# Weight words two pieces at a time, and eight of block 1's first products inside block 0's stage

## The chip, the cores and the metric

The kernel runs on one core of one Trainium2 chip. The metric is device microseconds for one execution, on that core. The core has a matrix engine (TensorE, in the trace PE, with its weight loads as PEld), a vector engine (VectorE, DVE), a scalar engine (ScalarE, ACT), GpSimd (POOL) and an engine that issues the data transfers (SyncE, SP). Each works through its own instructions in order, and semaphores tie them together.

## The reference

The input `x` is 2 sequences of 4096 tokens with 192 features. Three steps follow one another:

```
out = einsum('hk,bskhg->bshg', softmax(weight), windows of 7 tokens of x)   # causal convolution, 8 heads of 24
g, val = x @ w_gate, x @ w_val                                              # 192 -> 1536
x = (g * sigmoid(g) * val) @ w_out                                          # 1536 -> 192
h = x @ w_in                                                                # 192 -> 2048
g = where(h > 0, h, exp(min(h, 0)) - 1)
out = g @ w_out2                                                            # 2048 -> 192
```

The activations are float32; the five weight matrices of the two layers come as float64, that is as 64-bit words.

## The kernel before, in words

**Tiling.** The 8192 tokens are 16 blocks of 512. A block goes through layer 1 (gate, value, out) as one stage and through layer 2 (in, out) as another. The stages run in the order (1,0), (1,1), (1,2), (2,0), (2,1), (1,3), (2,2), (1,4), (2,3) and so on, the first number being the layer, the second the block. There are 14 places where layer 1 hands over to layer 2.

**Products.** Every float32 operand is split into a high and a low part of the type fp32r, and a product is the sum of three partial ones. The 192 rows of the contraction are handled as three slots of 64, and the matmuls go out in couples, one on the lower and one on the upper 64 rows. A unit of layer 1 (12 to a block) is `nine`: 18 matmuls of line 362 into the PSUM banks pg and pv. Then come silu of pg (ACT, line 672), the gate product with pv (DVE, line 676), the high part of the result (ACT, line 646) and its low part (DVE, line 650), which are called h. Then `ten`, 10 matmuls of line 405, adds h times the out weights into four banks c. In layer 2 a pair of units is one `nine` into two banks ph, with tanh and exp (ACT, lines 706 and 710), `less` and `bound` (DVE, lines 714 and 718), and the two parts of h for each of the two. pg, pv and ph share four PSUM banks (the ring "a"), so the `nine` after next writes the banks that silu and the gate product, or `bound`, must have read. The h parts have five buffers each.

Below, "OUT 3" is `ten` of unit 3 of a block, and a "first product" is a `nine`.

**Weights.** There are 34 pieces of 128 x 384 words. Pieces 0, 1, 3, 4, 6, 7, ... (12 of them) hold the gate and value columns of one unit of layer 1 (in1), pieces 2, 5, 8, ... the out rows of two units, and those from 18 on belong to layer 2. An in1 piece comes by four DMAs (line 262), as its upper and lower 64 rows have to change places; an out piece by one. Then ACT scales the high words (line 266) and takes the top bits of the low ones (line 289), DVE joins them and adds the sign (lines 293 and 274), ACT casts the high part (line 298) and DVE subtracts it for the low part (line 301). The words land in a ring `ws` of 4 buffers. A first product waits for both parts of its piece.

**Convolution.** For 128 of the 192 features a block's convolution is one multiply on ACT and six taps of 128x512 on DVE (line 576), then the split (lines 449 and 453). The last 64 features of blocks 0 and 1 go over PE (`pc`, line 552); from block 2 on, they are six more DVE taps of 128x256. The second copy of x with its halves turned around is made by DMAs (lines 490 and 496, issued on SP). Operands x and y live in three homes, each a pair of tiles for the high and the low part.

**Order.** The program lists every instruction as a task with a cost and what it needs. PE's tasks keep the order in which they were listed; on the other engines a planner picks, among the tasks that could start within 0.05 us of the first, the one with the longest work behind it. In the main loop a list `due` holds the units whose `ten` hasn't been listed: after each `nine`, all but the last entry of the list are worked off, so that OUT runs two units (or, in layer 2, two pairs) behind. At the end of a layer 1 stage the list is held for one step, and two OUTs follow after the first `nine` of layer 2.

Of the kernel before, what the change touches and what calls it, by code (L numbers as in the profile page):

```python
# [8 lines left out]
I32 = mybir.dt.int32  # L9
F32R = mybir.dt.float32r  # L10
# [6 lines left out]
P = 128  # L17
HALF = 64
TB = 512
SLOTS = (0, 2, 1)  # L20
LEAD = 3
AIDED = 1
PATIENCE = 0.05
EPS = 2.0**-16
SPARED = range(0, 34)

# [106 lines left out]
def tile_conv_swiglu_elu(ctx: ExitStack, tc: tile.TileContext, x, weight, words, out, FF1, FF2):  # L133
# [5 lines left out]
    nc = tc.nc  # L139
# [4 lines left out]
    NU = {1: FF1 // P, 2: FF2 // P}  # L144
    assert D == P + HALF and TB % 2 == 0
    C = 2 * D
# [5 lines left out]
    x_p = ctx.enter_context(tc.tile_pool(name="xp", bufs=1))  # L152
# [15 lines left out]
    plan = Plan()  # L168
# [10 lines left out]
    def move(emit, needs=(), new=(), uses=(), pitch=0.62, ready=2.9):  # L179
        return plan.add("sp", pitch, ready, emit, needs, new, uses)  # L180
# [65 lines left out]

    ready = {}

    def piece(k, moves, halves, serves):

        st_b, f_b = plan.buffer("ws", 4), plan.buffer("wf", 4)
# [10 lines left out]
        def scale():  # L264
            box["f"] = f = wf_p.tile([P, C], F32, tag="wf", name=f"w{k}")
            nc.scalar.activation(out=f, in_=box["st"][:, :, 1].bitcast(F32), func=AF.Abs, scale=2.0**-112)  # L266

# [16 lines left out]
        def three():  # L284

            w = box["st"].bitcast(U32)[:, :, 0]
            nc.scalar.activation(out=w, in_=w, func=AF.Copy, scale=2.0**-29 * (1 - EPS), bias=7.5 * EPS - 0.5)  # L289

# [12 lines left out]
        came = [  # L303
            move(lambda i=i: bring(i), new=[st_b] if i == 0 else (), uses=[] if i == 0 else [st_b], ready=3.3)
            for i in range(len(moves))
        ]
        for i in came[1:]:
            i.behind.append(came[0])
        t = act(scale, came, new=[f_b], uses=[st_b], pitch=0.45, ready=0.6)
        if k in SPARED:  # L310
            low_t = act(three, came, uses=[st_b], pitch=0.45, ready=0.6)
# [15 lines left out]
            ready[u] = his, los  # L327
        return came

    every, lower, upper = slice(0, P), slice(0, HALF), slice(HALF, P)  # L330

    class Into:


# [7 lines left out]
        def load(self, k, i):  # L342
            moves = (
                ((lower, slice(0, 3, 2)), (lower, slice(0, 3, 2))),
                ((lower, slice(1, 2)), (upper, slice(0, 1))),
                ((upper, slice(0, 3, 2)), (upper, slice(1, 3))),
                ((upper, slice(1, 2)), (lower, slice(1, 2))),
            )
            flat = lambda w: w[:, k].rearrange("p s c -> p (s c)")
            return piece(i, moves, [(lambda f: f, flat(self.hi), flat(self.lo))], [(self.name, k)])  # L350

        def nine(self, bufs, ps, k, x, n):

# [263 lines left out]
    live = {}  # L617
    parts = {}
    split_of = {}
    sums = {}  # L620
    turns = {"last": None}

# [10 lines left out]
    def split(u):  # L633

        layer, b, j = u
        n = blocks[b][2]
        t_b, done = live[u][1:]
        bufs = [plan.buffer(f"h{q}", 5) for q in ("hi", "lo")]
        parts[u] = [None, None]

        def make(q):
            parts[u][q] = h_p.tile([P, TB], F32R, tag=f"h{'hi lo'.split()[q]}", name=f"h{q}_{layer}_{b}_{j}")
# [12 lines left out]
        l = dve(lo, [done, h], new=[bufs[1]], uses=[bufs[0], t_b])  # L655
        split_of[u] = bufs, (h, l)
# [169 lines left out]
    products(1)  # L826
    load_table(AF.Silu)

    due = []
    for i, (layer, b) in enumerate(stages):  # L830
        if i + 1 < len(stages) and stages[i + 1][0] == 1:
            if i:
                load_x(stages[i + 1][1])
            conv(stages[i + 1][1], 0)
            if i >= AIDED:
                conv(stages[i + 1][1], 1)
        if i and stages[i - 1][0] != layer:
            load_table(AF.Silu if layer == 1 else AF.Exp)
        for j in range(0, NU[layer], layer):
            swiglu(b, j) if layer == 1 else elus(b, j // 2)  # L840

            hold = layer == 1 and j == NU[1] - 1 and i + 1 < len(stages) and stages[i + 1][0] == 2
            while len(due) > 1 and not hold:
                for u in due.pop(0):
                    products_out(u)
            due.append([(layer, b, j + a) for a in range(layer)])
    for us in due:
        for u in us:
            products_out(u)

    plan.run({"pe": 1.0, "act": 0.8, "dve": 1.0, "pool": 2.3, "sp": 0.8}, PATIENCE)


# [43 lines left out]
```

## Time and profile before

| | us |
|---|---|
| three runs of the kernel before | 1224.43 to 1225.32, median 1224.89 |
| the execution that was profiled | 1225.62 |
| its span, first to last instruction | 1223.9 |
| PE busy in the span | 1207.8 (99%) |
| DVE busy | 981.4 (80%) |
| ACT busy | 833.7 (68%) |

The profile comes from a single execution, with a span 1.72 us shorter than its device time. Times in the trace count from the first instruction of the span. The granted TensorE clock over the whole span was 0.997 of full speed. A matmul's row gives the time from its start to its modelled end; matmuls are pipelined, so that what counts is the distance between starts.

### The profile page before, as it was taken

What the parts mean: (1) busy time and instruction counts of PE and PEld (TensorE: products, weight loads), DVE (VectorE), ACT (ScalarE), POOL (GpSimd) and SP (SyncE); (2) the same over time, 40 slices, a digit from 0 to 9 for tenths busy, and PEclk for the clock granted to TensorE, in tenths of its full rate; (3) what the DMA queues carried; (4) which work ended last, traced back from release to release, by engine and by line L of the source; (5) the groups of instructions that cost most, each with busy time, mean ns of one, the idle gap of its engine ahead of it and who ended that gap; (6) DMA issues with size and microseconds to landing.
All of it is one profiled execution on the core that took longest, in us unless ns stands there. A gap on an engine that the chain in (4) does not pass through costs nothing.

```text
span 1223.9 us, 25338 instructions
## 1 busy us (share of the span) xinstructions
PE 1207.8 (99%) x10272; PEld 968.8 (79%) x10272; DVE 981.4 (80%) x1631; ACT 833.7 (68%) x1556; POOL 2.1 (0%) x15
## 2 busy tenths in 40 slices
PE   7999999999999999999999999999999999999998
PEld 5778888888888888788887888878878788888876
DVE  7999899788595986959779596895968869495697
ACT  6979687486583856748576484765848667485676
POOL 0000000000000000000000000000000000000000
PEclk9999999999999999999999999999999999999999
DMA  6644020202020020201102011020200102000000
GB/s 174 192 128 125 15 44 14 66 18 53 1 44 27 18 53 8 49 15 25 47 10 48 14 36 36 18 53 1 44 14 18 40 1 47 12 18 14 18 11 18
DMA packets 34917, 48.65 MB, mean 40 GB/s; under 512 B 5872, under 2 KB 19696, under 8 KB 34800
## 3 DMA queue, kind: packets, MB, share of 16 engines
q1 hardware_dynamic: 34784, 47.04, 15.1%
q8 instruction: 80, 1.31, 0.5%
q14 instruction: 37, 0.30, 0.1%
q10 hardware_dynamic: 16, 0.00, 0.0%
HBM read 19.75 MB, written 6.29 MB: 21 GB/s over the span
## 4 chain that ended last, share of the span: by engine, by line
PE 92%; DVE 3%; ACT 2%; SPq 1%; DMA 1%; issue 1%; ACTq 0%; DVEq 0%
PE c L405 40%; PE pv L362 30%; PE ph L362 21%; DMA words<-in_words_dram 1%; SPq L262 1%; DVE t L714 1%; DVE t L718 1%; PE pg L362 0%; DVE w L293 0%; DVE h L650 0%; ACT w L266 0%; DVE t L676 0%; ACT words L289 0%; SPq L518 0%; DVE in1lo L301 0%
## 5 line engine op out<-in xcount | busy, mean ns | idle before, releaser
L405 PE MATMUL c<-h,out 64*128 64x512 f32 x4480 | 639.4, 392 | 0.5 <-DVE o L755 0.4
L405 PEld LDWEIGHTS c<-h,out 64*128 64x128 f32 x4480 | 472.9, 185 | 104.6 <-DVE o L755 4.1
L646 ACT CAST h<-t 128x512 fp32r<-128x512 f32 x448 | 278.7, 623 | 175.3 <-DVE t L676 126.8
L362 PE MATMUL pg<-x,in1hi 64*128 64x512 f32 x1152 | 391.0, 393 | 2.9 <-ACT in1hi L298 2.3
L362 PE MATMUL pv<-x,in1hi 64*128 64x512 f32 x1152 | 391.1, 393 | 0.8 <-DVE t L676 0.8
L650 DVE TENSOR_TENSOR h<-t,h 128x512 fp32r<-128x512 f32 x448 | 307.6, 687 | 93.9 <-ACT h L646 91.2
L362 PE MATMUL ph<-y,in2hi 64*128 64x512 f32 x1536 | 317.6, 391 | 0.0
L362 PEld LDWEIGHTS ph<-y,in2hi 64*128 64x128 f32 x1536 | 236.7, 185 | 35.5 <-DVE t L718 0.6
L362 PEld LDWEIGHTS pv<-x,in1hi 64*128 64x128 f32 x1152 | 213.2, 185 | 49.3 <-DVE t L676 1.2
L362 PE MATMUL ph<-y,in2lo 64*128 64x512 f32 x768 | 238.3, 391 | 0.0
L362 PE MATMUL pg<-x,in1lo 64*128 64x512 f32 x576 | 226.7, 394 | 2.0 <-DVE in1lo L301 2.0
L676 DVE TENSOR_TENSOR t<-t,pv 128x512 f32<-128x512 f32 x192 | 131.3, 684 | 119.2 <-ACT t L672 119.0
L362 PE MATMUL pv<-x,in1lo 64*128 64x512 f32 x576 | 226.7, 394 | 0.0
L362 PEld LDWEIGHTS pg<-x,in1hi 64*128 64x128 f32 x1152 | 213.3, 185 | 7.5 <-ACT in1hi L298 4.1
L672 ACT ACTIVATE t<-pg 128x512 f32<-128x512 f32 x192 | 114.4, 596 | 148.1 <-PE pg L362 145.9
L714 DVE SCALAR_TENSOR_TENSOR t<-t,th 128x512 f32<-128x512 f32 x256 | 175.2, 685 | 9.8 <-ACT t L710 9.1
L718 DVE SCALAR_TENSOR_TENSOR t<-ph,t 128x512 f32<-128x512 f32 x256 | 171.8, 686 | 3.0
L706 ACT ACTIVATE th<-ph 128x512 f32<-128x512 f32 x256 | 153.7, 600 | 24.1 <-PE ph L362 23.1
L362 PEld LDWEIGHTS ph<-y,in2lo 64*128 64x128 f32 x768 | 141.2, 185 | 16.5
L710 ACT ACTIVATE t<-ph 128x512 f32<-128x512 f32 x256 | 154.0, 601 | 0.0
L362 PEld LDWEIGHTS pv<-x,in1lo 64*128 64x128 f32 x576 | 106.7, 185 | 24.4
L362 PEld LDWEIGHTS pg<-x,in1lo 64*128 64x128 f32 x576 | 106.7, 185 | 5.4 <-DVE in1lo L301 4.2
(56 smaller groups left out, 528.2 us busy)
## 6 DMA issues: line engine op xcount, KB each, us to landing
x<-x SPq DMA_DIRECT2D x64, 128.0 KB, 3.2
y<-y SPq DMA_DIRECT2D x64, 128.0 KB, 2.3
words<-in_words_dram SPq DMA_DIRECT2D x14, 384.0 KB, 3.4
words<-in_words_dram SPq DMA_DIRECT2D x40, 128.0 KB, 2.8
x<-x SPq DMA_DIRECT2D x64, 64.0 KB, 2.0
out_dram<-o SPq DMA_DIRECT2D x16, 256.0 KB, 2.0
xs<-in_x_dram SPq DMA_DIRECT2D x14, 259.0 KB, 3.1
words<-in_words_dram SPq DMA_DIRECT2D x40, 64.0 KB, 2.5
```

The source lines that it names most:

```text
L262: nc.sync.dma_start(out=to[r, g], in_=w[r_in, g_in])
L362: nc.tensor.matmul(p[:, :n], w[r, k, s], m[r, s, :n], start=i == 0, stop=i == len(seq) - 1)
L405: nc.tensor.matmul(p[:, :n], lhs[r], m[r, :n], start=start, stop=stop)
L646: nc.scalar.copy(parts[u][0][:, :n], live[u][0]["t"][:, :n])
L650: nc.vector.tensor_tensor(out=parts[u][1][:, :n], in0=live[u][0]["t"][:, :n], in1=raw(parts[u][0][:, :n]), op=ALU.subtract)
L672: nc.scalar.activation(out=box["t"][:, :n], in_=box["p"][0][:, :n], func=AF.Silu)
L676: nc.vector.tensor_tensor(out=t, in0=t, in1=box["p"][1][:, :n], op=ALU.mult)
L706: nc.scalar.activation(out=own["th"][:, :n], in_=box["p"][a][:, :n], func=AF.Tanh, scale=0.5)
L710: nc.scalar.activation(out=own["t"][:, :n], in_=box["p"][a][:, :n], func=AF.Exp)
L714: nc.vector.scalar_tensor_tensor(out=t, in0=t, scalar=1.0, in1=th, op0=ALU.add, op1=ALU.mult)
L718: nc.vector.scalar_tensor_tensor(out=t, in0=box["p"][a][:, :n], scalar=0.0, in1=t, op0=ALU.max, op1=ALU.min)
```

## The change

**Words by two.** The in1 pieces of the units 2 to 11 come in couples: a couple's words, 2 x 128 x 384, land by five DMAs in place of eight in one of the two tiles of the home that block 2's x will have, the couples taking turns between the two tiles. Both pieces of a couple wait for all five DMAs. Pieces 0 and 1 and the out pieces come as before.

**Block 1 in block 0's stage.** `both_first` lists the stages (1,0) and (1,1). Block 1's convolution is listed ahead of block 0's units. In block 0's stage OUT follows one `nine` behind. From unit 4 on (JOINED), each `nine` of block 0 is followed by one of block 1, so that units 0 to 7 of block 1 stand in block 0's stage. Their h parts don't go to the h ring but to the storage of in2's and out2's weights (`held`), and the pieces of layer 2 wait until those have been used (`give_back`). The transfer and convolution of block 2 are listed behind that. Then block 1's last four units follow, with two OUTs after each.

**Due.** `settle_due` works off at most two entries of the list after a `nine` of layer 1, and at most one after a `nine` of layer 2; an entry with a block's last unit ends the step.

```diff
+    def pair(k, which):
+        ring = ("xhi", "xlo")[which] + str(home["x", LEAD - 1])
+        st_b = plan.buffer(ring, 1)
...
+            at, r, g_in, row = (
+                (0, lower, 0, 0), (2, every, 2, 0), (0, upper, 1, HALF), (1, lower, 0, HALF), (1, upper, 1, 0)
+            )[i]
+            n = r.stop - r.start
+            source = words[k : k + 2, row : row + n, g_in * G2 : (g_in + 1) * G2].rearrange("e p c -> p e c")
+            nc.sync.dma_start(out=box["st"][r, :, at], in_=source)
...
+            if self.name == "in1" and k >= ALONE:
+                n, e = divmod(k - ALONE, 2)
+                if e == 0:
+                    self.pair = pair(i, n % 2)
+                shared = (*self.pair[:2], lambda view=self.pair[2]: view(e))
...
-        bufs = [plan.buffer(f"h{q}", 5) for q in ("hi", "lo")]
+        kept = u in held
+        bufs = [{"users": []} if kept else plan.buffer(f"h{q}", 5) for q in ("hi", "lo")]
...
+    for j in range(NU[1] - JOINED):
+        half = j // 2
+        held[1, 1, j] = (
+            ((spare[0][2], half), (spare[1][2], half)) if j % 2 == 0 else ((spare[2][2], j - 1), (spare[2][2], j))
+        )
...
+    def settle_due(most=2):
+
+        while len(due) > 1 and most:
+            us = due.pop(0)
+            for u in us:
+                products_out(u)
+            most = most - 1 if us[-1][2] < NU[us[-1][0]] - 1 else 0
+
+    def both_first():
+
+        conv(1, 0)
+        done = 0
+        waiting = []
+        for j in range(NU[1]):
+            swiglu(0, j)
+            if due:
+                for u in due.pop(0):
+                    products_out(u)
+            due.append([(1, 0, j)])
+            if j >= JOINED:
+                swiglu(1, done)
+                waiting.append([(1, 1, done)])
+                done += 1
+        load_x(2)
+        conv(2, 0)
+        conv(2, 1)
+        due.extend(waiting)
+        for j in range(done, NU[1]):
+            swiglu(1, j)
+            due.append([(1, 1, j)])
+            settle_due()
+
+    both_first()
     for i, (layer, b) in enumerate(stages):
+        if i < 2:
+            continue
...
-            while len(due) > 1 and not hold:
-                for u in due.pop(0):
-                    products_out(u)
+            if not hold:
+                settle_due(2 if layer == 1 else 1)
```

What moves on the engines is shown at three places. First DVE, from the low part of piece 0 (w0 is piece 0, w1 piece 1, w3 the piece of unit 2; cv1_0 is block 1's convolution, t1_0_0 unit 0 of block 0). Before:

```order
L301 TENSOR_TENSOR in1lo_115<-w0_189,in1hi_114 128x384
L576 SCALAR_TENSOR_TENSOR cv1_0_176<-xs1_143,taps_106,cv1_0_176 128x512
L477 TENSOR_TENSOR x11_243<-pc1_202,x10_235 64x256 x2
L301 TENSOR_TENSOR in1lo_115<-w1_216,in1hi_114 128x384
L293 SCALAR_TENSOR_TENSOR w3_250<-w3_250,words3_186 128x384
L274 SCALAR_TENSOR_TENSOR w3_250<-words3_186,w3_250 128x384
L576 SCALAR_TENSOR_TENSOR cv1_0_176<-xs1_143,taps_106,cv1_0_176 128x512
L301 TENSOR_TENSOR in1lo_115<-w3_250,in1hi_114 128x384
L576 SCALAR_TENSOR_TENSOR cv1_0_176<-xs1_143,taps_106,cv1_0_176 128x512 x2
L676 TENSOR_TENSOR t1_0_0_284<-t1_0_0_284,pv0_0_228 128x512
L576 SCALAR_TENSOR_TENSOR cv1_0_176<-xs1_143,taps_106,cv1_0_176 128x512
L650 TENSOR_TENSOR h1_1_0_0_317<-t1_0_0_284,h0_1_0_0_303 128x512
```

The same place now:

```order
L341 TENSOR_TENSOR in1lo_115<-w0_189,in1hi_114 128x384
L624 SCALAR_TENSOR_TENSOR cv1_0_176<-xs1_143,taps_106,cv1_0_176 128x512
L525 TENSOR_TENSOR x11_243<-pc1_202,x10_235 64x256 x2
L341 TENSOR_TENSOR in1lo_115<-w1_216,in1hi_114 128x384
L624 SCALAR_TENSOR_TENSOR cv1_0_176<-xs1_143,taps_106,cv1_0_176 128x512 x4
L730 TENSOR_TENSOR t1_0_0_277<-t1_0_0_277,pv0_0_228 128x512
L501 TENSOR_TENSOR x11_243<-cv1_0_176,x10_235 128x512
L704 TENSOR_TENSOR h1_1_0_0_304<-t1_0_0_277,h0_1_0_0_296 128x512
L333 SCALAR_TENSOR_TENSOR w3_301<-w3_301,words3_186 128x384
L312 SCALAR_TENSOR_TENSOR w3_301<-words3_186,w3_301 128x384
L730 TENSOR_TENSOR t1_0_1_314<-t1_0_1_314,pv0_1_271 128x512
```

All four remaining taps of block 1 (before: one, then two, then one, with piece 3 and the gate product between them) and the split of their sum now stand ahead of piece 3's join, and piece 3's low part has moved behind the second gate product.

Second, DVE in the middle of block 0's stage (t1_0_4 and t1_0_5 are units of block 0, w8 to w11 pieces). Before:

```order
L650 TENSOR_TENSOR h1_1_0_3_482<-t1_0_3_437,h0_1_0_3_469 128x512
L274 SCALAR_TENSOR_TENSOR w8_445<-words8_365,w8_445 128x384
L293 SCALAR_TENSOR_TENSOR w9_488<-w9_488,words9_390 128x384
L274 SCALAR_TENSOR_TENSOR w9_488<-words9_390,w9_488 128x384
L676 TENSOR_TENSOR t1_0_4_495<-t1_0_4_495,pv0_4_430 128x512
L301 TENSOR_TENSOR out1_118<-w8_445,out1_118 128x2x128
L301 TENSOR_TENSOR out1_118<-w8_445,out1_118 128x2x64
L301 TENSOR_TENSOR in1lo_115<-w9_488,in1hi_114 128x384
L293 SCALAR_TENSOR_TENSOR w10_530<-w10_530,words10_433 128x384
L274 SCALAR_TENSOR_TENSOR w10_530<-words10_433,w10_530 128x384
L650 TENSOR_TENSOR h1_1_0_4_560<-t1_0_4_495,h0_1_0_4_541 128x512
L676 TENSOR_TENSOR t1_0_5_546<-t1_0_5_546,pv0_5_485 128x512
```

Now, where t1_1_0 is unit 0 of block 1:

```order
L341 TENSOR_TENSOR out1_118<-w8_435,out1_118 128x2x64
L312 SCALAR_TENSOR_TENSOR w9_491<-words9_378,w9_491 128x384
L704 TENSOR_TENSOR h1_1_0_4_539<-t1_0_4_498,h0_1_0_4_524 128x512
L333 SCALAR_TENSOR_TENSOR w10_535<-w10_535,words9_378 128x384
L341 TENSOR_TENSOR in1lo_115<-w9_491,in1hi_114 128x384
L730 TENSOR_TENSOR t1_1_0_553<-t1_1_0_553,pv1_0_505 128x512
L312 SCALAR_TENSOR_TENSOR w10_535<-words9_378,w10_535 128x384
L333 SCALAR_TENSOR_TENSOR w11_567<-w11_567,words11_430 128x384
L312 SCALAR_TENSOR_TENSOR w11_567<-words11_430,w11_567 128x384
L730 TENSOR_TENSOR t1_0_5_589<-t1_0_5_589,pv0_5_542 128x512
L341 TENSOR_TENSOR in1lo_115<-w10_535,in1hi_114 128x384
L704 TENSOR_TENSOR in2lo_117<-t1_1_0_553,in2hi_116 128x512
```

A gate product and a low part of block 1 stand between those of block 0, and the low part's place is in2lo.

Third, PE where block 2 enters its layer 2, after the last couple of the first `nine` (ph2_0 and ph2_1; c1_3 are the banks of OUT for block 3's layer 1). Before, with two OUTs:

```order
L362 MATMUL ph2_1_3553<-y21_2305,in2hi_116 128x512
L405 MATMUL c1_3_2_3186<-h0_1_3_9_3499,out1_118 128x512
...
L405 MATMUL c1_3_3_3187<-h1_1_3_9_3507,out1_118 128x512
L405 MATMUL c1_3_2_3186<-h0_1_3_10_3536,out1_118 128x512
...
L405 MATMUL c1_3_3_3187<-h1_1_3_10_3544,out1_118 128x512
L362 MATMUL ph2_2_3609<-y20_2221,in2hi_116 128x512
```

Now:

```order
L410 MATMUL ph2_1_3517<-y21_2442,in2hi_116 128x512
L453 MATMUL c1_3_2_3153<-h0_1_3_9_3463,out1_118 128x512
...
L453 MATMUL c1_3_3_3154<-h1_1_3_9_3471,out1_118 128x512
L410 MATMUL ph2_2_3558<-y20_2225,in2hi_116 128x512
...
L410 MATMUL ph2_3_3559<-y21_2442,in2hi_116 128x512
L453 MATMUL c1_3_2_3153<-h0_1_3_10_3500,out1_118 128x512
```

One OUT stands between the first and the second `nine` of layer 2, where two stood; OUT 10 follows the second, and every later OUT of the stage stands one pair later than before. The last stage ends with eight OUTs behind its last `nine`, where six stood. At the step from layer 2 back to layer 1, four OUTs follow the first `nine` and two the second.

## Rows read from the trace of the kernel before

**Rows 1.** The page, part 1: busy us, share of the span, instructions per engine.
```profile
PE 1207.8 (99%) x10272; PEld 968.8 (79%) x10272; DVE 981.4 (80%) x1631; ACT 833.7 (68%) x1556; POOL 2.1 (0%) x15
```

**Rows 2.** Waits of PE: who waited for whom: us, times, longest us.
```profile
PE pg L362 <- ACT in1hi L298: 2.3, 3, 1.5
PE pg L362 <- DVE in1lo L301: 2.0, 5, 0.5
...
PE pv L362 <- DVE t L676: 0.8, 1, 0.8
PE pg L362 <- DMA x<-x: 0.5, 1, 0.5
```

**Rows 3.** Windows: length, busy us (instructions) by engine, PEclk, DMA share, GB/s.
```profile
core 0: us, PE busy (x) PEld busy (x) DVE busy (x) ACT busy (x) POOL busy (x), PEclk, DMA share, GB/s
15.40:31.20 15.80, 13.74 (x92) 10.19 (x92) 14.25 (x26) 10.07 (x23) 0.00 (x0) 0.89 0.66 179
16.30:19.60 3.30, 3.20 (x16) 2.63 (x17) 3.01 (x7) 1.85 (x5) 0.00 (x0) 0.50 0.75 167
31.20:74.70 43.50, 41.28 (x335) 31.45 (x337) 40.84 (x80) 37.39 (x79) 0.00 (x0) 1.00 0.54 153
50.00:60.00 10.00, 9.12 (x76) 6.72 (x74) 9.21 (x19) 9.24 (x21) 0.00 (x0) 1.00 0.75 218
74.70:152.00 77.30, 77.30 (x668) 62.54 (x666) 71.07 (x136) 58.38 (x120) 0.00 (x0) 1.00 0.34 94
152.00:231.00 79.00, 79.00 (x682) 63.72 (x680) 78.33 (x133) 59.87 (x114) 0.00 (x0) 1.00 0.18 43
74.70:1189.00 1114.30, 1114.30 (x9568) 896.93 (x9566) 887.13 (x1459) 752.72 (x1389) 0.13 (x2) 1.00 0.13 32
```

**Rows 4.** PE timeline of block 0: start us, us, line, [idle before <-releaser].
```profile
15.41 0.49 PE L362 MATMUL pg<-x,in1hi 64*128 64x512 f32 x1 [1.53 <-ACT in1hi L298]
...
23.10 0.49 PE L362 MATMUL pv<-x,in1hi 64*128 64x512 f32 x1 [0.77 <-DVE t L676]
...
25.06 1.56 PE L405 MATMUL c<-h,out 64*128 64x512 f32 x10
...
27.86 0.50 PE L362 MATMUL pg<-x,in1lo 64*128 64x512 f32 x1 [0.42 <-DVE in1lo L301]
```

**Rows 5.** DVE timeline from the first gate product on.
```profile
20.79 1.53 DVE L576 SCALAR_TENSOR_TENSOR cv<-xs,taps,cv 128x512 f32<-128x512 f32 x2
22.36 0.69 DVE L676 TENSOR_TENSOR t<-t,pv 128x512 f32<-128x512 f32 x1
22.96 0.75 DVE L576 SCALAR_TENSOR_TENSOR cv<-xs,taps,cv 128x512 f32<-128x512 f32 x1
23.73 0.69 DVE L650 TENSOR_TENSOR h<-t,h 128x512 fp32r<-128x512 f32 x1
...
25.11 0.56 DVE L293 SCALAR_TENSOR_TENSOR w<-w,words 128x384 int32<-128x384 int32 x1
25.70 0.56 DVE L274 SCALAR_TENSOR_TENSOR w<-words,w 128x384 int32<-128x384 int32 x1
```

**Rows 6.** SP timeline: DMA issues, start us, us, line, count.
```profile
15.78 1.87 SPq L496 DMA_DIRECT2D x<-x  x3
17.70 9.71 SPq L262 DMA_DIRECT2D words<-in_words_dram  x14
```

**Rows 7.** Timeline where block 2 enters its layer 2.
```profile
325.14 2.71 PE L405 MATMUL c<-h,out 64*128 64x512 f32 x20
...
327.46 0.61 PE L362 MATMUL ph<-y,in2hi 64*128 64x512 f32 x2
...
329.02 0.69 DVE L718 SCALAR_TENSOR_TENSOR t<-ph,t 128x512 f32<-128x512 f32 x1
```

**Rows 8.** Timeline after the last first product of layer 2.
```profile
1211.27 7.45 PE L405 MATMUL c<-h,out 64*128 64x512 f32 x60
...
1217.52 0.76 PEld L405 LDWEIGHTS c<-h,out 64*128 64x128 f32 x8 [0.26 <-DVE h L650]
```

More of the change, by code (lines that the diff above doesn't have):

```diff
@@ L23 @@
 PATIENCE = 0.05
+JOINED = 4
+ALONE = 2
 EPS = 2.0**-16
@@ L247, in tile_conv_swiglu_elu, with bring, piece @@
     ready = {}
-    def piece(k, moves, halves, serves):
-        st_b, f_b = plan.buffer("ws", 4), plan.buffer("wf", 4)
+    G2 = 2 * P
+    def pair(k, which):
+        ring = ("xhi", "xlo")[which] + str(home["x", LEAD - 1])
+        st_b = plan.buffer(ring, 1)
+        box = {}
+        def bring(i):
+            if i == 0:
+                full = x_p.tile([P, 3, TB], F32R, tag=f"x{which}{home['x', LEAD - 1]}", name=f"words{k}")
+                box["st"] = full.rearrange("p a b -> p (a b)").bitcast(I32).rearrange(
+                    "p (e g c) -> p e g c", e=2, g=3
+                )
[5 more added lines that the diff above has]
+            nc.sync.dma_start(out=box["st"][r, :, at], in_=source)
+        came = [
+            move(lambda i=i: bring(i), new=[st_b] if i == 0 else (), uses=[] if i == 0 else [st_b], ready=3.9)
+            for i in range(5)
+        ]
+        for i in came[1:]:
+            i.behind.append(came[0])
+        view = lambda e: box["st"][:, e].rearrange("p g (c w) -> p (g c) w", w=2)
+        return came, st_b, view
+    every, lower, upper = slice(0, P), slice(0, HALF), slice(HALF, P)
+    def piece(k, moves, halves, serves, shared=None):
+        st_b, f_b = shared[1] if shared else plan.buffer("ws", 4), plan.buffer("wf", 4)
         box = {}
@@ L264, in scale @@
         def scale():
+            if shared:
+                box["st"] = shared[2]()
             box["f"] = f = wf_p.tile([P, C], F32, tag="wf", name=f"w{k}")
@@ L284, in three @@
         def three():
+            if shared:
+                box["st"] = shared[2]()
             w = box["st"].bitcast(U32)[:, :, 0]
@@ L301, in lo_part @@
             nc.vector.tensor_tensor(out=lo, in0=pick(box["f"]), in1=raw(hi), op=ALU.subtract)
[L303 to L308, printed above, removed]
+        if shared:
+            came = shared[0]
+        else:
+            came = [
+                move(lambda i=i: bring(i), new=[st_b] if i == 0 else (), uses=[] if i == 0 else [st_b], ready=3.3)
+                for i in range(len(moves))
+            ]
+            for i in came[1:]:
+                i.behind.append(came[0])
         t = act(scale, came, new=[f_b], uses=[st_b], pitch=0.45, ready=0.6)
@@ L349, in load @@
             flat = lambda w: w[:, k].rearrange("p s c -> p (s c)")
-            return piece(i, moves, [(lambda f: f, flat(self.hi), flat(self.lo))], [(self.name, k)])
+            halves = [(lambda f: f, flat(self.hi), flat(self.lo))]
+            shared = None
+            if self.name == "in1" and k >= ALONE:
[3 more added lines that the diff above has]
+                shared = (*self.pair[:2], lambda view=self.pair[2]: view(e))
+            return piece(i, moves, halves, [(self.name, k)], shared)
         def nine(self, bufs, ps, k, x, n):
@@ L849, in tile_conv_swiglu_elu @@
             products_out(u)
+    give_back()
     plan.run({"pe": 1.0, "act": 0.8, "dve": 1.0, "pool": 2.3, "sp": 0.8}, PATIENCE)
```

23 lines of the change are left out of this document (22 added, 1 removed).

## The prediction

> **What bounds the kernel now.** I read the page first: PE is busy for 1207.8 of 1223.9 us [rows 1], so at most 16 us can be won without taking matmuls away, and the change takes none away. The windows say where these 16 us lie. From 74.70 to 1189.00 PE is busy without a break, 9568 matmuls at 0.1165 us each [rows 3]; there a change can only lose. Behind 1211.27 PE runs 60 matmuls, with 0.26 us of waiting [rows 8]. What is left is the start. From 15.40 to 31.20, 92 matmuls are worth 10.7 us and take 15.8, so 5.1 us are lost; from 31.20 to 74.70, 335 are worth 39.0 and take 43.5, so 4.5 are lost [rows 3]. These 9.6 us are what the change plays for.
>
> The table of PE's waits gives the causes by name: the high part of a weight piece 2.3 us, the low part 2.0, the gate product 0.8, the turned x 0.5 [rows 2]. They sum to 5.6, of which the 1.53 ahead of 15.41 lie outside the 9.6 [rows 4]; the remaining 5.5 are matmuls that start with a longer step though no wait is named. The largest such piece is the half clock: from 16.30 to 19.60 the granted clock is 0.50 (the 1.2 GHz level) and 3.3 us hold 16 matmuls [rows 3], where 0.1165 would allow 28; 12 x 0.1165 = 1.4 us. Behind the waits stands DVE: busy for 14.25 of the first 15.8 us and for 40.84 of the next 43.5 [rows 3]. Weight pieces, block 1's taps and the gate chain share it.
>
> **The start, to OUT 3.** Up to the low part of piece 1, the order of DVE and PE is as before, so PE's first two units and the half clock stay: from 15.41 on, part of their 36 matmuls run at half clock [rows 3], and they end at about 22, 6.5 us for 4.2, 2.3 lost. (In before unit 2 then waits for the gate product, to 23.10 [rows 4].)
>
> From there I chain by hand with the steps between starts on DVE: a tap behind its predecessor 0.78 (20.79 to 22.36 for two), a gate product 0.60 (22.36 to 22.96), a join with the sign behind it 0.59 (25.11 to 25.70) [rows 5]. Four taps, 3.1 us, now stand in one run ahead of the gate product of unit 0, where three taps and piece 3's join, sign and low part stood, 2.3 + 1.7. The gate product could come a little earlier for that; but its low part waits for ACT, which now casts x's split in front of it, and for DVE's own part of the split. I leave the gate product at 22.4 and the low part at 23.8 (before: 22.36 and 23.73 [rows 5]). OUT 0 now stands second in line and not behind unit 2, so PE starts it at 23.15 and waits for the low part; it ends at about 24.9 (before: 25.06 to 26.2 [rows 4]).
>
> Piece 3 comes with piece 4 by five transfers, two of them behind the x turns, which are issued until 17.65 [rows 6]; at 0.69 us per issue (9.71 / 14 [rows 6]) the last goes out at 19.0. That doesn't decide: DVE is free for piece 3's join at 24.3, behind the low part of unit 0, and 5 us should do for it to land. Join, sign, ACT's cast, and the low part behind the second gate product: unit 2 starts at 25.9, stands still for its low part to 26.85 and ends at 28.8. Here the new order is later than the old one, whose unit 2 ends at 25.06 [rows 4]. Then it makes good: piece 4 is done with piece 3, so unit 3 (old: stopped to 27.86 [rows 4]) runs from 29.96 without a stop, and units and OUTs follow one another at full rate: OUT 3 ends at 36.5.
>
> 130 matmuls stand before that point, worth 15.1 us; 36.5 - 15.4 = 21.1, so 6.0 us are lost. Against the 9.6 of before, 3.6 us are won if nothing is lost behind it. The uncertainty of the chain is one wait of each kind, +-1.5.
>
> **The rounds of block 0 and block 1.** From 36.5 PE has eight rounds of two units and one OUT, 46 matmuls or 5.36 us each, 42.9 together. Between the low part of unit 3 and the gate product of unit 7 of block 1, DVE has 81 instructions: 21 joins and signs, 14 low parts of pieces or halves of them, 31 gate products and low parts of h, 12 taps and 3 parts of block 2's x. At the steps of [rows 5], other widths in proportion to their columns, they add to some 41.3, with 1 to 2 more for steps that wait for the one before. So DVE is filled to the brim. Nothing on PE covers an idle microsecond of DVE there: behind a late low part stand OUT, then both units of the next round. The trace holds two stretches with DVE so full: 152 to 231, 78.33 of 79.00 busy and PE not waiting at all, and 31.20 to 74.70, 40.84 of 43.50 with 4.5 lost [rows 3]. So the cost lies between 0 and 4.5. It is nearer to the second in kind (pieces still arriving), but its waits for pieces are spread over more PE work per piece now; I take 1.2.
>
> The words are asked for in a burst: from about 27 (piece 4's sign frees the first tile) to piece 12 some 2.75 MB are queued. The join of piece 12 stands on DVE behind the gate product of unit 1 of block 1, at about 44. At the best ten microseconds' 218 GB/s the burst takes 12.6 us, at 153 it takes 18 [rows 3]: it is done at 40 or at 45.5, so 0 to 1.5 late. I take 0.3. The Trainium skill, DMA: Bandwidth & Descriptors, section Specifications, gives a limit of about 358 GB/s from HBM for a core; by that the burst would be through in an estimated 7.7 us and cost nothing, while no row here shows more than 218.
>
> `give_back` makes the pieces of layer 2 wait for OUTs of block 1. The work on DVE to the first `less` of (2,0) is the same, and between 74.70 and 152.00 DVE is idle for 77.3 - 71.1 = 6.2 us, which the earlier arrival can eat into [rows 3]; from 152 to 231 it is full in both. 0 to 0.5, I take 0.2.
>
> **The fourteen changes of layer.** Before, at T = 325.14 two OUTs begin; the second `nine` starts at 327.46 [rows 7], and the third, behind another OUT, 48 matmuls after T, at T + 5.6. Now one OUT lies between: the third `nine`, which writes the banks of the first, comes after 10 + 18 + 10 matmuls, at T + 4.4, its partner on the second bank 0.1 later. It needs the second `bound`, which runs from 329.02 for 0.69, to T + 4.57 [rows 7]. Before there was 1 us of room; now there is none. If DVE stays in step, 0 to 0.15 each; the steps behind it are as tight. I take 0.05, 0.7 us for 14. The cost if the cover is gone is in the rivals.
>
> At the end eight OUTs cover the last h parts instead of six, which removes the 0.26 [rows 8].
>
> **Sum:** 3.6 - 1.2 - 0.3 - 0.2 - 0.7 + 0.25 = about 1.4 us won. The profiled execution took 1225.62 (span 1223.9 and 1.72 around it), so 1224.2 by its own time; the median of the runs is 0.73 below it, and by that the forecast is 1223.5.
>
> **Rivals.** (1) *The start's gain comes through whole.* DVE stays ahead as it does from 152 to 231, and the fourteen changes cost nothing: 3.6 + 0.25 - 0.2 = 3.7, so 1221.2. For it: the pieces come earlier by couples and two units per round give each piece twice the PE work. Against: DVE's 41.3 plus dependent steps on 42.9.
>
> (2) *The clock falls a second time.* From 22.1 to 26.85 PE now has 12 matmuls, 1.4 us of work in 4.75. Before, the half clock of 16.30 followed on the idle 1.53 us [rows 3, 4]. Another such stretch costs the same 1.4 us, and the time is 1224.9. The Trainium skill, TensorE: Matmul & The Clock Gate, section Why this matters for your kernels, holds that idle gaps between bursts of matmuls send the engine back to half rate; the trace agrees at 16.30, and that rule speaks against the new order.
>
> (3) *Slower: the banks at the changes of layer.* If `exp`, `less` or `bound` slip by 0.35 us against PE (one DVE step that gets in between is 0.60), the third `nine` waits for `bound` at T + 5, and PE can't catch up: 0.4 x 14 = 5.6 us, against 2.1 won elsewhere: 1228.4. It decides from a second `bound` that ends later than T + 4.65. For it: room of 0.1 where 1 was. Against: the chain runs on ACT and DVE without waiting for PE's OUTs.
>
> (4) *The change does nothing.* DVE's work sets the start, in whatever order; the 3.6 are lost again by 80, the changes of layer cost 0.7: 1225.5.
>
> **Chances.** Forecast 0.42, rival 1 0.25, rival 2 0.15, rival 3 0.13, rival 4 0.05. The forecast's own range is 1222.0 to 1225.0. A measurement of this kernel can tell some 0.2% from no change, 2.45 us: faster than 1222.4 holds rival 1 nearly whole and the lower end of the forecast, 0.31; slower than 1227.3 rival 3 and a bad case of rival 4, 0.15; between them 0.54. The range from 1220.6 to 1228.0 leaves out the best part of rival 1 and the worse half of rival 3.
>
> **What would show it.** Right: OUT 3 ends at 36 to 37; from there PE's waits sum to 1 to 2 us; between 85 and 1189 PE's waits for `bound` are 14 short ones under 0.15. Wrong: a wait for `bound` of 0.3 and more at each change (rival 3); PEclk at 0.50 in 23 to 31 (rival 2); OUT 3 at 38 and later, which takes the gain away; or DVE with idle stretches in 40 to 75 while a `words` row is under way.

## The result, and the profile after

The changed kernel takes 1234.63 us (median of 5 runs, 1234.33 to 1235.93), the kernel before 1224.77 (1224.43 to 1225.32). The ratio is 1.0081, with a 95% interval of 1.0069 to 1.0093: it is slower by some 10 us, where 1.4 us of gain were forecast. The two profiled executions took 1235.93 and 1225.62 us, so the traces hold 10.3 us of difference.

The page, its first part and the costliest group, that of OUT's matmuls (after the bar: busy us, mean ns of one | idle before them and what ended most of it):

```profile
PE 1216.2 (99%) x10272; PEld 969.6 (79%) x10272; DVE 984.8 (80%) x1631; ACT 837.5 (68%) x1556; POOL 2.1 (0%) x15
...
L453 PE MATMUL c<-h,out 64*128 64x512 f32 x4400 | 629.5, 393 | 5.0 <-DVE o L809 1.9
```
PE is busy for 1216.2 us against 1207.8 [rows 1] with the same 10272 matmuls. A stretch in which one matmul waits while its neighbour is still running counts as busy, so most of the 10 us don't show as idle time. PE's waits (us, times, longest) name some of it:

```profile
PE c L453 <- DVE o L809: 1.9, 4, 0.5
PE c L453 <- ACT h L700: 1.7, 1, 1.7
PE pg L410 <- ACT in1hi L338: 1.2, 2, 0.8
...
PE c L453 <- DVE y L809: 0.8, 2, 0.6
PE pg L410 <- DVE in1lo L341: 0.6, 2, 0.5
...
PE ph L410 <- DVE t L772: 0.4, 2, 0.2
```
The waits for weight pieces have shrunk from 4.3 to 1.8 us [rows 2]. The 1.7 for h is the wait ahead of OUT 0, which now stands second in line. OUT's waits for `o` and `y` (DVE, line 809) have grown, from 0.4 and 0.2 us at one place each to 1.9 at four and 0.8 at two: these adds empty the banks c into which the next stage's first OUT writes. New are two waits of first products for `bound` (line 772). The windows tell when the time was lost (columns as in rows 3):

```profile
15.40:31.20 15.80, 12.60 (x70) 8.40 (x72) 13.56 (x24) 9.66 (x21) 0.00 (x0) 0.79 0.74 202
26.70:30.20 3.50, 3.45 (x16) 2.76 (x18) 2.94 (x6) 2.39 (x6) 0.00 (x0) 0.50 0.83 259
31.20:74.70 43.50, 43.09 (x365) 35.66 (x363) 40.50 (x79) 36.11 (x79) 0.00 (x0) 1.00 0.48 134
74.70:1189.00 1114.30, 1110.63 (x9472) 885.60 (x9470) 884.55 (x1449) 750.99 (x1378) 0.13 (x2) 1.00 0.13 32
```
To 74.70 the changed kernel is level with the old one: 70 + 365 matmuls against 92 + 335 [rows 3]. After it, PE starts 9472 matmuls in the 1114.30 us in which it started 9568 [rows 3], 96 fewer, or 11 us at 0.1165. Counting along the records of products from 15.4 us on gives the same: the 450th matmul starts 0.3 us earlier than before (76.96 against 77.29), the 9700th 11.1 us later (1165.91 against 1154.85). So the start isn't where the 10 us went, though of the 3.6 forecast to be won there 0.3 are left; the layers behind it are, where I had set 0.7 us.

**Where they lose it.** I took the time of each `nine` and each OUT from PE's records, from its start to that of the next, and subtracted 0.1163 us for each of its matmuls; what is left is called lost. Between 74.7 and 1190, first products of layer 2 lose 5.3 us and OUTs 7.6, together 12.9; before, the same count gives 2.2. 1.7 of the 12.9 lie at 85 and 112 us, in block 1 and block 2 (before: nothing; old_due, below, loses 0.6 there and only_due 1.0); no run takes them apart. Three places carry the rest.

(a) The third first product after each of the 14 changes to layer 2: 0.05 to 0.10 us each, 1.1 in all. This is the place of the prediction, and its price there was of the right size (0.7 in all).

(b) The sixth first product of the stage at the first twelve changes, 0.25 to 0.30 each, and the fourth at the last two, 0.46 each: 4.1 us. In the trace of after, block 3's stage:

```profile
420.10 0.68 DVE L768 SCALAR_TENSOR_TENSOR t<-t,th 128x512 f32<-128x512 f32 x1
...
420.81 0.69 DVE L772 SCALAR_TENSOR_TENSOR t<-ph,t 128x512 f32<-128x512 f32 x1
...
421.14 0.92 PE L410 MATMUL ph<-y,in2hi 64*128 64x512 f32 x2
...
421.56 0.73 PE L410 MATMUL ph<-y,in2lo 64*128 64x512 f32 x2
```
`bound` of the pair two before runs from 420.81 to 421.50. The first product that writes its banks begins at 421.14 with the matmul on the first bank; its next one, which waits for DVE, starts at 421.56, 0.06 us behind the end of `bound`, and the rest of the `nine` moves with it.

(c) The first OUT of a new stage of layer 1 after a change back, 0.2 to 0.8 us each (0.8 at the changes from 297 to 524, 0.2 to 0.3 at the other seven), and that of (2,1) at 187.6, some 5.9 us; before, the same places lose 1.5. After, at the fourth of them (p and o on line 809 empty the banks):

```profile
442.87 3.12 DVE L624 SCALAR_TENSOR_TENSOR cv<-xs,taps,cv 128x512 f32<-128x512 f32 x4
...
443.51 2.72 PE L453 MATMUL c<-h,out 64*128 64x512 f32 x20
...
445.90 0.68 DVE L730 TENSOR_TENSOR t<-t,pv 128x512 f32<-128x512 f32 x1
446.49 1.00 DVE L624 SCALAR_TENSOR_TENSOR cv<-xs,taps,cv 128x256 f32<-128x256 f32 x2
...
447.41 0.68 DVE L809 TENSOR_TENSOR p<-p,c 128x512 f32<-128x512 f32 x1
...
447.93 0.94 PE L453 MATMUL c<-h,out 64*128 64x512 f32 x5
...
448.61 0.68 DVE L809 TENSOR_TENSOR o<-o,c 128x512 f32<-128x512 f32 x1
...
449.34 0.95 PE L453 MATMUL c<-h,out 64*128 64x512 f32 x5 [0.47 <-DVE o L809]
```
Before, at the same place:

```profile
437.48 0.75 DVE L576 SCALAR_TENSOR_TENSOR cv<-xs,taps,cv 128x512 f32<-128x512 f32 x1
...
438.23 2.72 PE L405 MATMUL c<-h,out 64*128 64x512 f32 x20
...
438.75 1.53 DVE L576 SCALAR_TENSOR_TENSOR cv<-xs,taps,cv 128x512 f32<-128x512 f32 x2
...
440.20 0.68 DVE L676 TENSOR_TENSOR t<-t,pv 128x512 f32<-128x512 f32 x1
...
440.80 0.74 DVE L576 SCALAR_TENSOR_TENSOR cv<-xs,taps,cv 128x512 f32<-128x512 f32 x1
...
441.46 0.68 DVE L755 TENSOR_TENSOR p<-p,c 128x512 f32<-128x512 f32 x1
...
442.65 1.70 PE L405 MATMUL c<-h,out 64*128 64x512 f32 x10
442.66 0.68 DVE L755 TENSOR_TENSOR o<-o,c 128x512 f32<-128x512 f32 x1
```
The last two OUTs of layer 2 begin at 438.23 and 443.51; 4.4 us later, behind one `nine`, stands the first OUT of layer 1. Before, p's add starts 3.2 us and o's add 4.4 us after them, and OUT is held for 0.15. After, with four taps of 128x512 and two of 128x256 ahead in place of three and one of 128x512, it is 3.9 and 5.1: OUT does five matmuls from 447.93 and gets to the next five at 449.34.

### The profile page after: what moved, and what is told of

Its sections match the earlier page's. It is cut to its first block, busy times and chain, and to the rows that moved or that the text cites. A ratio compares the mean times of both kernels' runs of the same rounds, so it can differ in the third digit from the quotient of the medians.

```text
span 1234.2 us, 25366 instructions
## 1 busy us (share of the span) xinstructions
PE 1216.2 (99%) x10272; PEld 969.6 (79%) x10272; DVE 984.8 (80%) x1631; ACT 837.5 (68%) x1556; POOL 2.1 (0%) x15
## 4 chain that ended last, share of the span: by engine, by line
PE 79%; DVE 15%; ACT 2%; issue 2%; DMA 1%; SPq 1%; DVEq 0%; ACTq 0%
PE c L453 34%; PE pv L410 25%; PE ph L410 20%; DVE h L704 3%; DVE cv L624 3%; DVE t L768 2%; DVE t L772 2%; DVE t L730 1%; DMA words<-in_words_dram 1%; PE pg L410 1%; SPq L272 1%; DVE x L525 1%; DVE p L809 0%; ACT L192 0%; DVE x L501 0%
## 5 line engine op out<-in xcount | busy, mean ns | idle before, releaser
L453 PE MATMUL c<-h,out 64*128 64x512 f32 x4400 | 629.5, 393 | 5.0 <-DVE o L809 1.9
L453 PEld LDWEIGHTS c<-h,out 64*128 64x128 f32 x4400 | 465.0, 185 | 108.8 <-DVE o L809 7.0
L700 ACT CAST h<-t 128x512 fp32r<-128x512 f32 x440 | 274.7, 627 | 175.7 <-DVE t L730 124.9
L704 DVE TENSOR_TENSOR h<-t,h 128x512 fp32r<-128x512 f32 x440 | 292.9, 685 | 88.6 <-ACT h L700 88.1
L410 PE MATMUL ph<-y,in2hi 64*128 64x512 f32 x1536 | 322.5, 393 | 0.4 <-DVE t L772 0.4
L410 PE MATMUL ph<-y,in2lo 64*128 64x512 f32 x768 | 240.9, 395 | 0.0
L624 DVE SCALAR_TENSOR_TENSOR cv<-xs,taps,cv 128x512 f32<-128x512 f32 (+1 forms) x180 | 107.8, 620 | 1.8
```

Source lines behind the costliest of these rows:

```text
L410: nc.tensor.matmul(p[:, :n], w[r, k, s], m[r, s, :n], start=i == 0, stop=i == len(seq) - 1)
L453: nc.tensor.matmul(p[:, :n], lhs[r], m[r, :n], start=start, stop=stop)
L624: nc.vector.scalar_tensor_tensor(out=acc, in0=s, scalar=w, in1=acc, op0=ALU.mult, op1=ALU.add)
L704: nc.vector.tensor_tensor(out=parts[u][1][:, :n], in0=live[u][0]["t"][:, :n], in1=raw(parts[u][0][:, :n]), op=ALU.subtract)
```

## The experiments

Ratios are against runs of the kernel before on the same chip.

**Is it the rule for `due`?** Two kernels: the change with the old rule, and the old kernel with the new rule alone.

```diff
 (old_due, in the changed kernel)
-            if not hold:
-                settle_due(2 if layer == 1 else 1)
+            while len(due) > 1 and not hold:
+                for u in due.pop(0):
+                    products_out(u)
 (only_due: the reverse, in the kernel before, with settle_due defined there)
```

> The changed kernel, with the list `due` worked off by the old rule (all but the last entry after each first product) in all stages from (1,2) on; the words by two and block 1 inside block 0's stage stay. Theory A (the 10 us were lost after the start, by OUT running one pair later in layer 2): PE's progress stays that of the changed kernel to about 75 us, and the 11.4 us lost from there on go, so 1223.3 to 1225.0 us, the kernel before within 0.15%. Rival B (the loss after 75 us comes from the new places of operands and weights, or from layer 2's pieces being held back): 1230 or more.

> The kernel before with the new rule for `due` alone (two entries after a first product of layer 1, one after one of layer 2), and the old start. Theory A: the loss is all there, 10 to 12 us over before, so 1234.5 to 1237 us, with PE waiting 0.06 to 0.09 and 0.25 to 0.30 us in two first products at each of the 14 changes from layer 1 to 2, and 0.2 to 0.8 us in the first OUT of layer 1 after each change back. Rival B: 1225 to 1227 us.

old_due: 1225.45 us, ratio 1.0000 (0.9990 to 1.0009). only_due: 1235.87 us, ratio 1.0081 (1.0066 to 1.0096). The windows of old_due, then of only_due:

```profile
31.20:74.70 43.50, 43.50 (x376) 35.70 (x374) 42.35 (x82) 36.82 (x80) 0.00 (x0) 1.00 0.46 130
74.70:1189.00 1114.30, 1113.69 (x9560) 899.51 (x9559) 887.62 (x1460) 754.23 (x1392) 0.13 (x2) 1.00 0.13 32
```
```profile
31.20:74.70 43.50, 41.45 (x341) 32.20 (x339) 40.43 (x78) 36.50 (x78) 0.00 (x0) 1.00 0.57 158
74.70:1189.00 1114.30, 1110.40 (x9480) 887.16 (x9480) 884.91 (x1448) 750.20 (x1378) 0.13 (x2) 1.00 0.13 32
```
With the old rule 9560 matmuls start behind 74.70, with the new one 9480. The whole loss comes with the rule and goes with it; the words by two and block 1's early units neither cause it nor are needed for it. Theory A stands, rival B is out. old_due also shows what the rest of the change is worth: 376 matmuls in 31.20 to 74.70 against 335 [rows 3], though it is behind at 31.20; on the clock, nothing that the interval would show.

**Which part of the rule's cost lies where?** early_lag has OUT one pair late only in the first half of a layer 2 stage, late_lag only at its end.

```diff
 (early_lag)
-                settle_due(2 if layer == 1 else 1)
+                settle_due(2 if layer == 1 or j >= 8 else 1)
... (late_lag, layer 2 alone)
+                n = 1 if j in (6, 12) and i + 1 < len(stages) and stages[i + 1][0] == 1 else 2
+                while n and len(due) > 1:
+                    products_out(due[0].pop(0))
+                    if not due[0]:
+                        due.pop(0)
+                    n -= 1
```

> The changed kernel, but in layer 2 the list is caught up at the fifth first product (two entries from there on), so that OUT is one pair late only in the first half of a layer 2 stage, and the change back to layer 1 is as in the kernel before. Theory A in parts: the waits of first products for `bound` at the 14 changes to layer 2 stay (5.3 us by the changed kernel's trace), those of OUT for the banks c go (5.7 us): some 5 us over the run with the old rule, 1228 to 1230 us. If both have one cause (OUT being late as such) it is 1224 or 1235.

> The changed kernel, but a layer 2 stage that is followed by layer 1 begins with the old rule and gives up one OUT after its fourth and one after its seventh first product, so that OUT is one pair late only at the change back to layer 1 (four OUTs after the first unit, two after the second). Theory A in parts: only the waits of OUT for the banks c are there, 5.7 us by the changed kernel's trace, 1229 to 1231 us, if the two short steps inside the stage cost nothing; up to 0.5 us a stage more if they do.

early_lag: 1235.96 us (1.0079, 1.0062 to 1.0096). late_lag: 1233.04 us (1.0057, 1.0042 to 1.0072). Both miss, early_lag by 6 us and late_lag by 2. In early_lag the waits at the changes to layer 2 are there in part (0.06 to 0.10 each at the third first product, none at the sixth, 0.5 at the fourth of the last two changes), but at each of the ten changes back from 296 us on the first OUT of layer 1 loses 0.8 to 1.0 us, though OUT there stands exactly where it stood before. By its time alone early_lag would have borne out the other reading, that OUT being late costs the same wherever it is late (1235); the places of the waits speak against it. In late_lag the waits of (a) and (b) are gone but for two of under 0.1 us, the two short steps inside the stage cost nothing, and ten changes back lose 0.7 to 0.95 each, together more than in the changed kernel. The trace of early_lag at that place:

```profile
442.47 2.71 PE L453 MATMUL c<-h,out 64*128 64x512 f32 x20
...
443.02 2.33 DVE L624 SCALAR_TENSOR_TENSOR cv<-xs,taps,cv 128x512 f32<-128x512 f32 x3
...
445.27 0.68 DVE L730 TENSOR_TENSOR t<-t,pv 128x512 f32<-128x512 f32 x1
...
445.86 0.75 DVE L624 SCALAR_TENSOR_TENSOR cv<-xs,taps,cv 128x512 f32<-128x512 f32 x1
...
446.52 0.68 DVE L809 TENSOR_TENSOR p<-p,c 128x512 f32<-128x512 f32 x1
...
446.89 1.10 PE L453 MATMUL c<-h,out 64*128 64x512 f32 x5
```
Three taps stand ahead of a gate product on DVE, one more between it and p's add. As many stand there before, but there the first begins 0.75 us ahead of the two OUTs, here 0.55 behind their start, and p's add comes 4.05 us behind that start (before: 3.2). The order on DVE is the planner's: with OUT moved elsewhere, its reckoning of what is ready when came out otherwise. That points away from the place of OUT as the cause of (c), and to what stands ahead of two adds on DVE.

**Is it the order on DVE?** gather_first keeps the change, new rule and all, and tells the planner that all but the first two taps of the block being convolved come behind the two adds. early_gather has the same condition in early_lag. The comments say what the two lists hold.

```diff
...
+    for b, adds in adds_of.items():                # adds_of[b]: finish's adds of p and o
+        for late in taps_of.get(b + 4, [])[2:]:    # taps_of[b]: the DVE taps of conv(b, 0) and conv(b, 1)
+            late.behind += adds
```

> The changed kernel, new rule for `due` and all, with one more condition for the planner: at a change from layer 2 to 1, all taps but the first two of the block that is then being convolved come after the two DVE adds that empty the banks c. Theory (the first OUT of layer 1 waits because taps stand ahead of these adds on DVE): the wait of 0.2 to 0.8 us at each change back falls to 0.3 or less, 2 to 4 us in all, 1230.5 to 1232.5; the waits of first products in layer 2 (5.3 us) stay. Rival (OUT is simply too late, whatever DVE does first): 1234 to 1236.

> early_lag (OUT one pair late only in the first half of a layer 2 stage) with the condition of gather_first (the adds that empty the banks c before the taps). In early_lag PE lost 0.95 to 0.99 us at each change back to layer 1, with OUT in its old place there. Theory (the loss there is the planner's order on DVE, which the lag has moved, and not OUT's place): these waits fall to 0.3 or less, 1226 to 1228. Rival (the banks are freed late for another reason): 1233 to 1236.

gather_first: 1230.93 us (1.0042, 1.0027 to 1.0058). early_gather: 1229.39 us (1.0031, 1.0019 to 1.0043). In gather_first the waits from the change back at 297 us on are gone (none over 0.05 us); those at 188 and 222 us stay (0.8 and 0.4), and those of (a) and (b) are all there:

```profile
442.15 2.72 PE L453 MATMUL c<-h,out 64*128 64x512 f32 x20
...
444.97 0.68 DVE L811 TENSOR_TENSOR p<-p,c 128x512 f32<-128x512 f32 x1
...
445.56 0.68 DVE L811 TENSOR_TENSOR o<-o,c 128x512 f32<-128x512 f32 x1
...
446.57 0.39 PE L410 MATMUL pv<-x,in1hi 64*128 64x512 f32 x1
446.57 1.55 PE L453 MATMUL c<-h,out 64*128 64x512 f32 x10
```
OUT runs its ten matmuls from 446.57 without a stop, as p's and o's adds begin 2.8 and 3.4 us behind the start of the two OUTs. In early_gather the change back costs 0.13 to 0.29 at all but one place (0.51) instead of 0.8 to 1.0; it lands 1.4 us above the range that I gave. So (c) is, from 297 us on, the planner's order, some 4 us of it in the change and 6.5 in early_lag. The part of (b) at the sixth first product goes with OUT being late in the whole stage (it is in only_due and gather_first and not in early_lag); what exactly pushes `bound` there was not tried by itself, and its cause stays open.

**The start.** Three kernels on old_due: no_join has JOINED = 12 (no unit of block 1 in block 0's stage), no_pair has ALONE = 12 (no couples of words), and warm lets PE do idle 64-row matmuls where it waits.

```diff
 (warm: seven between unit 1 and OUT 0, three between OUT 0 and unit 2, on a bank of ring "a")
...
+            nc.tensor.matmul(box["p"][:, :TB], W1.hi[lower, 0, 0], X[0].tiles[0][lower, 0, :TB], start=True, stop=True)
```

> The changed kernel with the old rule for `due`, and with JOINED at 12: no unit of block 1 stands in block 0's stage, the words still come by two, block 1's taps still stand early, OUT is one unit behind in block 0. By the sum on record the gain of the start comes from block 1's units filling PE's waits: without them PE waits for pieces from 36 us on, 3 to 5 us more than old_due by 75 us, so 1227 to 1230. If the couples of words alone bring the gain: 1224 to 1225.5.

> The changed kernel with the old rule for `due`, and with ALONE at 12: every piece's words come by their own four transfers, block 1's units stand in block 0's stage as in the change. If the couples matter little: within 1 us of old_due, 1224 to 1226.5, with unit 2 earlier (piece 3 doesn't share its transfers) and later pieces up to 1.5 us later. If 30 more transfers on SP hold up the pieces: PE loses 2 to 4 us more before 75 us, 1227 to 1229.

> The changed kernel with the old rule for `due` from stage (1,2) on (as in old_due), and with idle matmuls that nobody reads: seven 64-row ones on a free PSUM bank between unit 1 and OUT 0, three between OUT 0 and unit 2, where PE waits anyway. Clock theory (the start's gain was spent on a second stretch at half clock, 26 to 31 us): PEclk stays near 1.00 in 23 to 31, unit 2 ends at about 29 and not at 30.3, PE is 2 to 2.5 us ahead of old_due at 36, and 1 to 2.5 at 75 us, so 1222 to 1224. Rival (DVE sets the pace of the start, the clock was hidden): PE is ahead at 36 and back at old_due's place at 75, 1224 to 1225.5.

no_join: 1228.84 us (1.0026, 1.0017 to 1.0035), 3.4 over old_due (344 matmuls in 31.20 to 74.70 against 376): block 1's units do fill PE's waits. no_pair: 1225.36 us (0.9999, 0.9990 to 1.0008), no difference from old_due that can be told. warm: 1225.42 us (1.0001, 0.9992 to 1.0010). In its profile the clock is where it was asked to be, and it brought nothing:

```profile
26.70:30.20 3.50, 3.39 (x30) 2.77 (x32) 3.50 (x8) 3.50 (x10) 0.00 (x0) 1.00 0.85 231
40.00:45.00 5.00, 4.05 (x36) 2.94 (x32) 1.79 (x4) 1.48 (x4) 0.00 (x0) 1.00 0.81 184
```
From 26.70 to 30.20 the clock is 1.00, and 30 matmuls start where the changed kernel started 16. At 39 us PE is 2.1 us ahead of old_due. From 40 to 45 DVE is busy for 1.79 us, and ACT's timeline says why:

```profile
43.73 0.54 ACT L329 ACTIVATE words<-words 128x384 uint32<-128x384 uint32 x1 [3.52 <-DMA words<-in_words_dram]
44.17 0.60 ACT L700 CAST in2hi<-t 128x512 fp32r<-128x512 f32 x1
44.68 0.59 ACT L726 ACTIVATE t<-pg 128x512 f32<-128x512 f32 x1
```
ACT stands for 3.5 us before it can take the low words of pieces 12 and 13 (line 329), with the cast and silu of units that have long been done queued behind. PE starts 36 matmuls from 40 to 45, and 46 in old_due. Behind this sparse stretch the clock falls again: from 47.40 to 50.80 it is 0.50, with 20 matmuls against 32 in old_due at 1.00. Together this takes back more than the 2.1 us: the 450th matmul starts 1.7 us later than in old_due (77.2 against 75.5). So the gain was handed over to the transfers and, through the gap that they make, to the clock once more; the rival was right that it doesn't last, with DMA in the place of DVE. gather_first, which has no idle matmuls, shows the same when PE comes early: 36 matmuls from 40 to 45, and 0.50 behind them.

One profile is one execution. Over all executions the mean granted clock of the whole span is 0.9971 in old_due (ten) and 0.9984 in warm (eleven); in late_words and warm_late, which follow below and differ by the idle matmuls alone, it is 0.9971 and 0.9986. So the idle matmuls do raise it.

**Transfers in another order.** late_words (on old_due) and warm_late (on warm) issue the out pieces 14 and 17 and block 2's x behind pieces 12 and 13; best has gather_first's condition too.

```diff
+    for i in (14, 17):
+        moves_of[i][0].behind.append(moves_of[12][-1])
...
         load_x(2)
+        xs[2][2][0][-1].behind.append(moves_of[12][-1])
```

> As old_due (the changed kernel with the old rule for `due`), with the transfers of out pieces 14 and 17 and of block 2's x issued behind those of pieces 12 and 13, which are needed sooner. In old_due ACT waits 0.7 us for words between 30 and 80 us, so by itself it brings little: within 1 us of old_due, 1223.5 to 1226.

> late_words and the idle matmuls of warm together. Theory (in warm, ACT stood 3.5 us behind the words of pieces 12 and 13 with unit 5's silu queued behind, and that took back the 2 us that the clock gave): the wait for words falls under 1.5 us, PE is 2 us or more ahead of old_due at 45 us, and at 75 us still 1 to 2: 1221.5 to 1224. Rival (the queue is full of other transfers, or DVE sets the pace anyway): back at old_due's place or behind it by 75 us, 1224 to 1226.

> warm_late with the condition of gather_first, so with the old rule for `due`: the kernel that the runs so far point to. The old rule leaves 11 waits of 0.15 us at the changes back to layer 1, so the condition is worth 0 to 1.5 us: 1220.5 to 1224, faster than the kernel before by 0.1 to 0.4%. Rival (the condition moves taps into the way of first products of layer 1): 1224 to 1227.

late_words: 1225.05 us (0.9995, 0.9986 to 1.0004). warm_late: 1223.84 us (0.9989, 0.9980 to 0.9998). best: 1221.93 us against 1225.50 for the kernel before (0.9974, 0.9965 to 0.9983), 0.26% faster than the kernel before and 1% faster than the changed one. Windows of best, whose 96 matmuls up to 31.20 include the ten idle ones:

```profile
15.40:31.20 15.80, 14.20 (x96) 10.17 (x98) 15.10 (x28) 11.14 (x25) 0.00 (x0) 1.00 0.80 202
31.20:74.70 43.50, 43.50 (x375) 34.80 (x373) 41.75 (x82) 35.99 (x78) 0.00 (x0) 1.00 0.48 135
74.70:1189.00 1114.30, 1113.35 (x9568) 902.68 (x9566) 888.53 (x1462) 755.28 (x1394) 0.13 (x2) 1.00 0.13 32
```
In warm_late and best ACT's waits for words between 30 and 80 us are 2.4 and 2.0 us, none of them longer than 1.3, and OUT 3 ends at 36.4. 86 + 375 matmuls of the kernel's own start before 74.70 where it was 92 + 335, and behind it as many start as before the change. The waits of 0.08 to 0.16 us that warm_late still has at the changes back from 291 us on are gone in best.

No run has best without the idle matmuls, or the condition of gather_first alone on old_due. late_words and warm_late differ by the idle matmuls alone; 1.2 us lie between them, and their intervals overlap. In four of best's eleven executions the mean clock is 1.000, in the others 0.997 to 0.999, and those are no slower (1222.0 the median of the four, 1221.9 that of the five at 0.998). So what each part of best is worth is not shown, only what they are worth together.

## Why the prediction was wrong

- **The fourteen changes of layer: the step that failed.** The prediction weighed one wait, that of the third first product for the second `bound`, and forecast 0.05 us each, 0.7 in all. That wait came, at 0.05 to 0.10 (1.1 in all). But the same rule moves every later OUT of the stage by a pair, and I priced nothing behind the third first product, though the sentence "the steps behind it are as tight" stood there; it cost 4.1 us, at the sixth above all. And the changes from layer 2 back to layer 1, whose new order the text ahead of the prediction describes, had no term at all: 5.9 us, where it was 1.5 before. Together 11 us are lost there, 9.6 more than before, against a forecast of 0.7.
- **Rival 3** named the right part of the change and the wrong wait. Its price, 0.4 at each of 14, was near the sum of (a) and (b), its time of 1228.4 was 6 us short, above all as (c) is missing from it and as the 2.1 us won elsewhere didn't come. I took the order on DVE at these places as given, since DVE's instructions are the same; the planner had rearranged it.
- **The start, to OUT 3.** The hand chain was right to 0.1 us as far as the clock held: OUT 0 at 23.14 (23.15 forecast), unit 2 at 25.80 (25.9), its low part at 26.75 (26.85). Then rival 2 came in:

```profile
23.14 0.49 PE L453 MATMUL c<-h,out 64*128 64x512 f32 x2 [1.72 <-ACT h L700]
...
25.80 0.79 PE L410 MATMUL pg<-x,in1hi 64*128 64x512 f32 x1 [0.49 <-ACT in1hi L338]
...
26.75 0.79 PE L410 MATMUL pg<-x,in1lo 64*128 64x512 f32 x1 [0.16 <-DVE in1lo L341]
...
30.34 1.84 PE L453 MATMUL c<-h,out 64*128 64x512 f32 x10
```
Unit 2 ends at 30.34 and not at 28.8, at a granted clock of 0.50 from 26.70 to 30.20, and OUT 3 ends at 38.5 and not at 36.5. That is 2.0 us, more than rival 2's 1.4: the low clock lasts from 24.60 to 31.50 (0.51), 6.9 us against the 3.3 of before. The stretch at half clock of 16.30 to 19.60 in before [rows 3] isn't in the traces of after and old_due, where the clock is 1.00 there; that gave back 0.9 us by the 18th matmul. Where the clock is at 1.00 from 23 to 31, OUT 3 ends at 36.4, as the chain had it: with the idle matmuls (warm_late, best), and without them in late_words and gather_first, whose low stretch lies at 16 to 20, ahead of the wait for OUT 0.
- **The rule of the Trainium skill** (TensorE: Matmul & The Clock Gate, section Why this matters for your kernels), that idle gaps between bursts send the engine back to half rate, points the right way on the new order: the clock fell after the 1.72 us before OUT 0 and in the sparse stretch behind it. With these filled it is at 1.00 there in warm, warm_late and best. But the profiles don't bear it out simply: in late_words and gather_first, unfilled, the sparse stretch passes at 1.00, behind a fall near 16 to 17, while early_lag and no_join, unfilled too, fall at both places.
- **Rounds of block 0 and block 1, words in a burst.** 1.2 and 0.3 us were forecast. After 38.5 us the changed kernel loses 1.2 us to 65 (0.2, 0.1, 0.8 and 0.1 at four places). The burst of words costs nothing there, as PE is late by 2 us; where PE comes on time it costs all of that, with the second fall of the clock that it brings (warm). The clock of rival 2 and the burst were taken as separate terms, and they cover each other. The 0.2 for layer 2's pieces can't be told apart; 1.7 us are lost at 85 and 112 us, of open cause.
- **Rival 1**, the start's gain whole (3.6), is what warm_late and best show: the 400th matmul starts 3.3 to 3.6 us earlier than before. Neither warm nor late_words has it in its time; the two together, with the condition of gather_first, are 3.6 us faster than the kernel before.

## What to carry to other kernels

A rule that is changed for the start and also used in a steady loop must be priced in the loop: here 0.5 to 1.2 us in each of 14 rounds outweighed everything at the start. When a planner orders the queues, moving one engine's work can rearrange another engine at a place that the edit doesn't touch; compare the order on every engine at each boundary between stages, above all what stands ahead of the instructions that free a buffer. And where several things are late within the same few microseconds (clock, transfers, DVE), taking one away shows only the next: try them together before calling a gain hidden.

## What the runs showed of the hardware that wasn't expected

The low clock moves between executions of nearly the same program: in 16.30 to 19.60 the granted clock is 1.00 in the profiles of after and old_due and 0.62 in that of late_words, and in 26.70 to 30.20 it is 0.50 in the first two and 1.00 in the third. Up to 75 us each of these three has one such stretch, and it isn't of one length: 24.60 to 31.50 is at 0.51 in after and old_due. Others have two, early_lag and no_join at 16.30 to 19.60 (0.58, 0.57) and 26.70 to 30.20 (0.55, 0.54). Where it falls moved PE's place at 39 us by 2.1 us: the matmul that starts at 39.17 in before starts 1.67 later in old_due and 0.45 earlier in late_words. A low stretch at 16 to 20 costs little there, since PE then waits in any case for the h of OUT 0, which starts at 23.14 or 23.15 in all three.
